# Weight combinations in small pieces, and eight units of the last product converted in the second layer

## The chip, the cores and the metric

One core of a Trainium2 chip runs the kernel. The metric is the device time of one execution in microseconds (us). Engines are called TensorE (PE in the profile; PEld is its weight load), VectorE (DVE), ScalarE (ACT), GpSimd (POOL) and SyncE (SP), whose queue issues the DMAs spoken of here.

## The reference

A retention layer feeds a two-layer network of 2304 tokens by 512 features:

```python
scores = scale * np.matmul(q, k.transpose(0, 1, 3, 2))     # 4 batches, 8 heads, 576 tokens, 64 features
x = np.matmul(scores * Dmat, v)                            # Dmat: gamma ** distance, causal
h = x @ w_in                                               # first layer, 512 -> 2048
x = (h * np.tanh(softplus(h))) @ w_out                     # mish, 2048 -> 512
g, val = x @ w_gate, x @ w_val                             # second layer, 512 -> 1536, twice
out = (g * (1 / (1 + np.exp(-g))) * val) @ w_out2          # 1536 -> 512, "the last product"
```

The inputs q, k and v are float32; the weights come as float64.

## The kernel before

**Numbers.** A float32 value is held as two parts, a rounded one and the rest, and a matrix product is three matmuls for each pair of tiles. The float64 weights are decoded on the chip. A raw tile (512 KB, 128 partitions of 512 doubles) is loaded, `rebias_raw` (L112) scales the high words on ScalarE (L114) and shifts the low ones on VectorE (L115), `sign` (L117, L119) and `join` (L121, L123) put them together on VectorE, and a cast on ScalarE and a subtraction on VectorE or GpSimd make the two parts (`part`, L125, for the first layer's units).

**Work of TensorE.** The tokens are six blocks of 384. After the retention (which already holds slots 0 to 3), the first layer runs blocks 0 to 3 in 64 *slots*, 16 to a block: a slot is 12 matmuls `g1` (L615) and, four slots later, 12 matmuls `g2` (L649) that add to four PSUM banks. At a block's end `g2_out` (L654, L659) copies the banks out, two on ScalarE and two on VectorE, before the next block may fill them. Blocks 4 and 5 go together through eight *pairs* (`pair1`, L888): two by two weight units are multiplied with seven block products instead of eight. A pair has seven *steps*; in a step one product (six matmuls, L813) is followed by some matmuls of waiting accumulations (L826, L855). The second layer runs all of its 18 *units* (three token pairs times six weight pairs) in this form, each with a gate half (z = 0) and a value half (z = 1) of seven steps (`strassen`, L1027), the accumulations of the last product (L989) in between. In a step the first product goes to a copy on ScalarE (L921 or L1061), and most of the others to an add on VectorE (L820) that reads the bank; two PSUM banks serve the three sums of a half in turn.

**Weights for it.** The seven products need combinations of weights: for a group of two weight units, four corner pieces a11 to a22 (128 x 256 x 2) and sums s1 to s4, of which seven are used. They are made while the first layer runs, and stored in device memory: `put` (L189) casts a piece on ScalarE (L191), subtracts on VectorE (L192) and stores (L193) from a pool "c" of four buffers. There are

- twelve groups of gate and value weights, `group(n)` (L203): load two raw tiles, decode, four sums (`combine`, L199, L201), seven stores into `comb`;
- eight groups of first-layer weights, `group1(i)` (L231): add the two parts of units that are there already (L246), four sums, four stores `e_s` and three straight from the units, into `ecomb`;
- twelve units of the last product, `last(i)` (L259): load, decode, two casts with subtractions on GpSimd, two stores into `find`, from which `fin_load` (L736) loads them in the second layer.

**Order.** The program is in the order in which it is written (no scheduler); each engine takes its instructions in turn. `pieces()` (L273) yields this work as 154 pieces, each made of whole stages (both rebiases of a group; three stores, then two, then two). `second` (L303) is called at the end of each slot from slot 20 on (L704) and of each step of the pairs (L942), and makes pieces until their number is 2.6 for each slot and 1.15 for each step. Raw tiles come from one ring of four buffers (`rp`). Functions in the list `ahead` split inputs of the next stage, one or two to a step; for the second layer from step 34 on. `stream1` and `stream` (L724, L734) load the combinations into a ring of weight tiles ahead of the products, six in the pairs and nine in the second layer.

Of the kernel before, what the change touches and what calls it, by code (L numbers as in the profile page):

```python
# [16 lines left out]
def retention_mish_swiglu(  # L17
# [34 lines left out]
    RATE, RATE1, AHEAD = 2.6, 1.15, 34  # L52
# [6 lines left out]
    rp = cr.enter_context(tc.tile_pool(name="rp", bufs=RAW, side="right"))  # L59
# [34 lines left out]
    def fetch(lim):  # L94
        j = stage[0]
        if j >= min(lim, len(todo)) or j - stage[3] >= RAW:
            return
        stage[0] += 1
        kind, i, src = todo[j]
        raw[j] = rp.tile([128, 2 * DM], U32, tag="raw", name=f"raw{j}")  # L100
        dst = raw[j] if kind in ("out", "fin") else raw[j].rearrange("p (k f) -> p k f", k=KT)
        nc.sync.dma_start(out=dst, in_=src)
# [81 lines left out]
    def raw_load(key, src, whole):  # L184
        raw[key] = rp.tile([128, 2 * DM], U32, tag="raw", name=f"raw{key}")
# [13 lines left out]
    def combine(v):  # L199
        for o, a, b, op in ADDS:  # L200
            nc.vector.tensor_tensor(out=v[o], in0=v[a], in1=v[b], op=op)  # L201

    def group(n):  # L203
# [4 lines left out]
        def load():  # L208
            for e in range(2):
                raw_load(keys[e], cols((w2_gate, w2_val)[z], 2 * i + e), False)  # L210

        def bias():
            for e in range(2):
                rebias_raw(keys[e])

        def whole(e):
            sign(keys[e])
            join(keys[e])
            lo, hi = words(keys[e])
            for h in range(2):  # L220
                v[f"a{e + 1}{h + 1}"] = lo[:, h * KH:(h + 1) * KH].bitcast(F32)
                v["s" + "1324"[2 * e + h]] = hi[:, h * KH:(h + 1) * KH].bitcast(F32)

        def puts(names):
# [4 lines left out]
        return load, bias, whole, lambda: combine(v), puts  # L229

    def group1(i):  # L231
        v = {}

        def whole():
            x = rp.tile([128, 2 * DM], U32, tag="raw", name=f"e{i}").bitcast(F32)
# [16 lines left out]
        def puts(names):  # L252
# [4 lines left out]
        return whole, lambda: combine(v), puts  # L257

    def last(i):  # L259
        key = f"f{i}"  # L260

        def whole():
            sign(key)
            join(key)
# [6 lines left out]
        return lambda: raw_load(key, rows(w2_out, i), True), lambda: rebias_raw(key), whole, puts  # L271

    def pieces():  # L273
        gr = [group(n) for n in range(2 * PAIRS)]
        yield gr[0][0]
        yield lambda: None
        for n in range(2 * PAIRS):
            load, bias, whole, sums, puts = gr[n]
            f_load, f_bias, f_whole, f_puts = last(n)
            g = group1(n) if n < F1 // 2 else None  # L280
            yield bias
            yield lambda: (whole(0), f_load())
            if g:
                yield g[0]
            yield lambda: whole(1)
            if g:
                yield g[1]
            yield sums
            yield lambda: puts(("a11", "a12", "a22"))
            if g:  # L290
                yield lambda: g[2](("s2", "s3"))
            yield lambda: puts(("s2", "s3"))
            yield lambda: (puts(("s1", "s4")), gr[n + 1][0]() if n + 1 < 2 * PAIRS else None)
            if g:
                yield lambda: g[2](("s1", "s4"))
            yield f_bias
            yield f_whole
            yield f_puts

    prep = pieces()  # L300
    made = [0]

    def second(lim):  # L303
        while made[0] < lim:
            made[0] += 1
            f = next(prep, None)
            if f is None:
                return
            f()
# [298 lines left out]
    with tc.manual_schedule():  # L608
# [70 lines left out]
        def slot(s):  # L679
# [23 lines left out]
            if s >= PREP:  # L703
                second(int((s + 1 - PREP) * RATE))  # L704
# [14 lines left out]
        ring2 = ring1[cut:] + ring1[:cut] + [("in", 9), None, None]  # L719
# [437 lines left out]
```

## Time and profile before

| | us |
|---|---|
| median of 3 runs (lowest to highest) | 936.55 (936.43 to 938.25) |
| the profiled execution | 935.03 |
| its span, first to last instruction | 933.2 |
| TensorE busy (share) | 910.6 (98%) |
| VectorE busy | 568.0 (61%) |
| ScalarE busy | 380.0 (41%) |
| GpSimd busy | 70.0 (8%) |
| granted clock, mean | 0.996 |

The profile is one execution, with every instruction's start and duration; a busy TensorE is not one at its peak, since matmuls overlap. "Idle before" an instruction is put down to the semaphore that came last. Stages by time from the span's start: retention to 105 us, slots to 361 us, pairs to 509 us, second layer to the end.

### The profile page before, as it was taken

To read this page: it belongs to the slowest core of one execution; us is meant where nothing else is said; L and a number is where in the kernel's file an instruction comes from. 1 tells how busy PE (TensorE), PEld (TensorE's weight loads), DVE (VectorE), ACT (ScalarE), POOL (GpSimd) and SP (SyncE) were. 2 spreads that over 40 slices of the span, in tenths; PEclk is the share of its full clock that TensorE was granted. 3 is DMA by queue.
4 is the path that set the end of the run, shared out by engine and by line. 5 is a ranking of instruction groups with operands and counts; after the bars stand their busy time and mean duration, and the time that the engine had idled before them with its cause. 6 is when DMAs were issued, how large, how long until landed. Compare 5 with 4: busy or idle time off the path is not lost.

```text
span 933.2 us, 15315 instructions
## 1 busy us (share of the span) xinstructions
PE 910.6 (98%) x5828; PEld 863.5 (93%) x5828; DVE 568.0 (61%) x1086; ACT 380.0 (41%) x798; POOL 70.0 (8%) x71
## 2 busy tenths in 40 slices
PE   9999999999999997999999999999999999999998
PEld 8888999999899997899999999999999999999997
DVE  3978599467767787777653544556544556544444
ACT  3877466355554555545443222223222223222222
POOL 3654100000000000000000000000000000000000
PEclk9999999999999999999999999999999999999999
DMA  9999265277776779989635666654644554644421
GB/s 219 258 251 219 74 199 176 62 237 230 254 255 213 240 251 303 317 300 321 216 125 216 242 203 204 203 168 154 227 163 159 157 164 156 228 158 158 159 68 67
DMA packets 130520, 185.97 MB, mean 199 GB/s; under 512 B 46736, under 2 KB 88464, under 8 KB 130448
## 3 DMA queue, kind: packets, MB, share of 16 engines
q1 hardware_dynamic: 129344, 184.58, 63.0%
q8 instruction: 46, 0.75, 0.3%
q10 hardware_dynamic: 1104, 0.42, 0.2%
q14 instruction: 26, 0.21, 0.1%
HBM read 137.26 MB, written 47.71 MB: 198 GB/s over the span
## 4 chain that ended last, share of the span: by engine, by line
PE 72%; DMA 10%; DVE 10%; ACT 4%; issue 2%; SPq 1%; POOL 0%; DVEq 0%; ACTq 0%; POOLq 0%
PE t L813 28%; PE fa L989 16%; PE h L615 7%; PE acc L649 6%; PE ea L855 5%; PE te L813 4%; DMA comb<-c 3%; DMA rawg<-in_moe_w_gate_dram 2%; DMA eu<-ecomb 2%; DMA rawv<-in_moe_w_val_dram 1%; PE o L518 1%; DMA raw<-in_moe_w_out_dram 1%; PE s L442 1%; DVE c L192 1%; DVE g L677 1%
## 5 line engine op out<-in xcount | busy, mean ns | idle before, releaser
L813 PE MATMUL t<-y,su 128*128 128x384 f32 x1512 | 306.3, 338 | 0.5 <-DVE cv L820 0.5
L813 PEld LDWEIGHTS t<-y,su 128*128 128x128 f32 x1512 | 270.6, 188 | 23.7 <-DVE cv L820 1.9
L989 PE MATMUL fa<-fu,g 128*128 128x512 f32 x648 | 190.3, 395 | 0.2 <-ACT g L1012 0.2
L615 PE MATMUL h<-xs,u 128*128 128x384 f32 x768 | 144.0, 337 | 0.7 <-DVE xs L325 0.7
L649 PE MATMUL acc<-g,u 128*128 128x384 f32 x720 | 135.0, 336 | 3.8 <-ACT y L659 3.5
L615 PEld LDWEIGHTS h<-xs,u 128*128 128x128 f32 x768 | 133.9, 188 | 1.5 <-DVE xs L325 1.0
L649 PEld LDWEIGHTS acc<-g,u 128*128 128x128 f32 x720 | 125.5, 188 | 5.2 <-ACT y L659 4.2
L989 PEld LDWEIGHTS fa<-fu,g 128*128 128x128 f32 x648 | 118.5, 188 | 7.8 <-ACT g L1012 0.5
L1012 ACT CAST g<-sg 128x384 fp32r<-128x384 f32 x72 | 36.9, 513 | 173.6 <-DVE sg L1048 120.3
L813 PE MATMUL te<-ye,eu 128*128 128x384 f32 x336 | 69.8, 343 | 9.3 <-ACT scratch L921 6.1
L855 PE MATMUL ea<-ge,u 128*128 128x256 f32 x576 | 78.1, 282 | 0.2 <-ACT y L659 0.2
L855 PEld LDWEIGHTS ea<-ge,u 128*128 128x128 f32 x576 | 75.6, 189 | 0.9 <-DVE y L659 0.4
L1037 ACT ACTIVATE sg<-sg 128x384 f32<-128x384 f32 x54 | 28.4, 525 | 100.1 <-DVE sg L820 100.1
L813 PEld LDWEIGHTS te<-ye,eu 128*128 128x128 f32 x336 | 57.5, 191 | 11.5 <-ACT scratch L921 6.4
L1017 DVE TENSOR_TENSOR g<-sg,g 128x384 fp32r<-128x384 f32 x72 | 40.2, 558 | 40.6 <-ACT g L1012 40.6
L677 DVE TENSOR_TENSOR g<-m,g 128x384 fp32r<-128x384 f32 x64 | 36.1, 565 | 36.7 <-ACT g L673 36.5
L820 DVE TENSOR_TENSOR u<-t,p 128x384 f32<-128x384 f32 x36 | 20.0, 556 | 48.0 <-PE t L813 43.6
L666 ACT ACTIVATE m<-h 128x384 f32<-128x384 f32 x64 | 31.0, 485 | 38.0 <-PE h L615 37.9
L820 DVE TENSOR_TENSOR v<-t,p 128x384 f32<-128x384 f32 x36 | 20.0, 556 | 41.9 <-PE t L813 41.2
L192 POOL TENSOR_TENSOR f<-rawf,f 128x256 fp32r<-128x256 f32 x24 | 18.9, 811 | 337.7 <-ACT f L191 267.2
L673 ACT CAST g<-m 128x384 fp32r<-128x384 f32 x64 | 32.9, 514 | 1.8
L1048 DVE TENSOR_TENSOR sg<-sg,cv 128x384 f32<-128x384 f32 x54 | 30.1, 558 | 1.9
(115 smaller groups left out, 991.7 us busy)
## 6 DMA issues: line engine op xcount, KB each, us to landing
su<-comb SPq DMA_DIRECT2D x126, 512.0 KB, 3.3
comb<-c SPq DMA_DIRECT2D x84, 256.0 KB, 2.4
eu<-ecomb SPq DMA_DIRECT2D x28, 512.0 KB, 5.4
raw<-in_moe_w_in_dram SPq DMA_DIRECT2D x16, 512.0 KB, 5.4
raw<-in_moe_w_out_dram SPq DMA_DIRECT2D x16, 512.0 KB, 3.9
ecomb<-e_s SPq DMA_DIRECT2D x32, 256.0 KB, 4.4
rawg<-in_moe_w_gate_dram SPq DMA_DIRECT2D x12, 512.0 KB, 6.2
rawf<-in_moe_w_out_dram SPq DMA_DIRECT2D x12, 512.0 KB, 6.0
```

The source lines that it names most:

```text
L615: nc.tensor.matmul(ps, lhsT=u[:, a, kk * 128:(kk + 1) * 128], rhs=s[:, e, :], start=(c == 0), stop=(c == n - 1),)
L649: nc.tensor.matmul(accs[b][d][:, :T], lhsT=u[:, a, d * 128:(d + 1) * 128], rhs=g[:, e, :], start=(i == 0 and c == 0), stop=(i == F1 - 1 an ...
L666: nc.scalar.activation(w, hs.pop(s), AF.Mish)
L673: nc.scalar.copy(out=gs[s][:, 0, :], in_=ws[s])
L677: nc.vector.tensor_tensor(out=g[:, 1, :], in0=ws.pop(s), in1=g[:, 0, :].bitcast(F32), op=ALU.subtract)
L813: nc.tensor.matmul(p, lhsT=w[:, a, kk * 128:(kk + 1) * 128], rhs=y[kk][:, x, :], start=begin and kk == 0 and (a, x) == (0, 0), stop=kk == ...
L820: nc.vector.tensor_tensor(out=out_, in0=a, in1=b_, op=ALU.add)
L855: nc.tensor.matmul(o, lhsT=u[:, a, d * 128:(d + 1) * 128], rhs=y, start=f == 0 and (a, x) == (0, 0) and (r == 0 or r == 2 and d % 2 == 0), ...
L989: nc.tensor.matmul(accs["f", b][m], lhsT=gs[u, e, h][:, x, m * 128:(m + 1) * 128], rhs=fu[2 * (u % PAIRS) + e][:, a, :], start=first, stop ...
L1012: nc.scalar.copy(out=gs[u, e, h][:, 0, :], in_=x)
L1017: nc.vector.tensor_tensor(out=g[:, 1, :], in0=x, in1=g[:, 0, :].bitcast(F32), op=ALU.subtract)
L1048: later.append(lambda: nc.vector.tensor_tensor(out=y, in0=y, in1=x, op=ALU.mult))
```

## The change

- The groups' work is dealt out by cost. Each piece has a cost (about its time on VectorE in us) and holds one conversion or at most two stores; `Pace` gives every slot or step a budget and makes pieces while the budget covers the next one's cost.
- Gate and value groups and `last` get 2.0 for each slot from 20, 1.2 from slot 51, and 1.2 for each step of pairs 1 to 7; none in pair 0. The groups of first-layer weights have a list of their own, 1.0 for each slot.
- The ring of raw tiles becomes four tiles with one buffer and one user each (two for a group, one for `last`, one for `group1`).
- Only units 0 to 3 of the last product are still made in the first layer (`FIRST = 4`). Units 4 to 11 are loaded raw in the second layer and converted by `fin_step` in the gate halves of units 1 to 4, one or two operations to a step, on VectorE and ScalarE, straight into their tiles. Behind groups 4 to 11 stand two empty pieces instead.
- The raw tiles of that take the place of a tile of the ring of weights (eight instead of nine). The split of inputs for the second layer starts at step 45 instead of 34, two to a step.

```diff
-    RATE, RATE1, AHEAD = 2.6, 1.15, 34
+    RATES, AHEAD = (2.0, 1.2, 1.2, 1.0), 45
...
-    def raw_load(key, src, whole):
-        raw[key] = rp.tile([128, 2 * DM], U32, tag="raw", name=f"raw{key}")
+    def raw_load(key, src, whole, n):
+        raw[key] = rp.tile([128, 2 * DM], U32, tag=f"raw{n}", name=f"raw{key}")
...
-        return load, bias, whole, lambda: combine(v), puts
+        return load, [
+            (0.55, lambda: rebias_raw(keys[0])), (0.55, lambda: rebias_raw(keys[1])),
+            (0.7, lambda: sign(keys[0])), (0.7, lambda: join(keys[0])),
+            (0.7, lambda: sign(keys[1])), (0.7, lambda: join(keys[1])),
+            (0.85, lambda: puts("a11", "a12")), (0.85, lambda: combine(v, ("s1", "s3"))),
+            (0.45, lambda: puts("a22")), (0.85, lambda: combine(v, ("s2", "s4"))),
+            (0.85, lambda: puts("s1", "s3")), (0.85, lambda: puts("s2", "s4")),
+        ]
...
-        return whole, lambda: combine(v), puts
+        return [
+            (1.4, whole), (0.85, lambda: combine(v, ("s1", "s3"))), (0.85, lambda: puts("s1", "s3")),
+            (0.85, lambda: combine(v, ("s2", "s4"))), (0.85, lambda: puts("s2", "s4")),
+        ]
+
+    FIRST = 4
...
+        gap = [(0.8, lambda: None)] * 2
+        for n, (load, steps_) in enumerate(gr):
+            f_load, behind = last(n) if n < FIRST else (None, gap)
+            if n == 0:
+                yield 0.0, load
+                yield from gap
+            yield from steps_[:2]
+            if f_load:
+                yield 0.0, f_load
+            yield from steps_[2:]
+            if n + 1 < len(gr):
+                yield 0.0, gr[n + 1][0]
+            yield from behind
+
+    class Pace:
+        def __init__(self, todo_):
+            self.todo, self.left, self.ahead = todo_, 0.0, next(todo_, None)
+
+        def __call__(self, more):
+            self.left += more
+            while self.ahead and self.left >= self.ahead[0]:
+                self.left -= self.ahead[0]
+                self.ahead[1]()
+                self.ahead = next(self.todo, None)
+
+    second = Pace(pieces())
+    third = Pace(x for i in range(F1 // 2) for x in group1(i))
...
-                second(int((s + 1 - PREP) * RATE))
+                third(RATES[3])
+                second(RATES[s >= NS - F1 + 3])
...
-        ring2 = ring1[cut:] + ring1[:cut] + [("in", 9), None, None]
+        ring2 = ring1[cut:] + ring1[:cut] + [None, None]
...
+        def fin_step(u, c):
+            n = FIRST + 2 * (u - 1)
+            i, k = divmod(c, 4) if c < 4 else (1, c - 3)
+            i += n
+            key = f"f{i}"
+            if k == 0:
+                rebias_raw(key)
+            elif k == 1:
+                sign(key)
+            elif k == 2:
+                join(key)
+                fin_load(i)
+                nc.scalar.copy(out=fu[i][:, 0, :], in_=words(key)[0].bitcast(F32))
+            else:
+                nc.vector.tensor_tensor(
+                    out=fu[i][:, 1, :], in0=words(key)[0].bitcast(F32), in1=fu[i][:, 0, :].bitcast(F32), op=ALU.subtract
+                )
+                fin_raw(i + 2)
+            if c == 3:
+                rebias_raw(f"f{n + 1}")
...
-                    pop(ahead, 1)
-                second(int((NS - PREP) * RATE + (step + 1) * RATE1))
+                    pop(ahead, 2)
+                if i:
+                    second(RATES[2])
...
-        fin_load(0)
-        fin_load(1)
+        for i in range(FIRST):
+            fin_load(i)
+        fin_raw(FIRST)
+        fin_raw(FIRST + 1)
...
+                if z == 0 and 0 < u <= (F2 - FIRST) // 2:
+                    fin_step(u, c)
```

ScalarE, slots 33 to 35, at the end of the second block of tokens, before. `m` and `g` are a slot's own mish and cast, `c` and `e_s` the casts of stores, `y` the block's copies out of PSUM:

```order
L666 ACTIVATE m_2888<-h_2863 128x384
L673 CAST g_2890<-m_2888 128x384
L191 CAST c_0_2893<-rawg_0_2691 128x256
L191 CAST c_2_2897<-rawg_0_2691 128x256
L191 CAST c_5_2901<-rawg_1_2693 128x256
L191 CAST e_s_2905<-e_2818 128x256
L191 CAST e_s_2909<-e_2818 128x256
L191 CAST c_1_2913<-rawg_1_2693 128x256
L191 CAST c_3_2917<-rawg_0_2691 128x256
L666 ACTIVATE m_2946<-h_2921 128x384
L673 CAST g_2890<-m_2946 128x384
L659 COPY y_2950<-acc_0_2251 128x384
```

The same place after:

```order
L661 ACTIVATE m_2900<-h_2875 128x384
L668 CAST g_2902<-m_2900 128x384
L191 CAST e_s_2905<-e_2713 128x256
L191 CAST e_s_2909<-e_2713 128x256
L191 CAST c_5_2915<-rawg_1_2737 128x256
L661 ACTIVATE m_2944<-h_2919 128x384
L668 CAST g_2902<-m_2944 128x384
L654 COPY y_2948<-acc_0_2251 128x384
L654 COPY y_2948<-acc_2_2253 128x384
L191 CAST c_4_2961<-rawg_0_2735 128x256
```

Seven casts for stores stood ahead of the block's copies, and three do now.

ScalarE at the entry into the pairs, before. `scratch` takes the first product of pair 0, `f` and `rawf` belong to a unit of the last product, `ye` to the pairs' inputs:

```order
L666 ACTIVATE m_4285<-h_4260 128x384
L673 CAST g_4235<-m_4285 128x384
L114 ACTIVATE rawf_4085<-rawf_4085 128x512
L191 CAST f_0_4293<-rawf_4085 128x256
L191 CAST f_1_4297<-rawf_4085 128x256
L921 COPY scratch<-te_1_4304 128x384
L766 CAST ye_0_4318<-x_1202 128x384
L766 CAST ye_1_4319<-x_1202 128x384
L114 ACTIVATE rawg_0_4246<-rawg_0_4246 128x512
```

And after:

```order
L661 ACTIVATE m_4199<-h_4174 128x384
L668 CAST g_4167<-m_4199 128x384
L114 ACTIVATE rawv_1_4099<-rawv_1_4099 128x512
L947 COPY scratch<-te_1_4209 128x384
L792 CAST ye_0_4223<-x_1202 128x384
L792 CAST ye_1_4224<-x_1202 128x384
L792 CAST ye_0_4245<-t_e 128x384
L792 CAST ye_1_4246<-t_e 128x384
L923 ACTIVATE we_4257<-te_1_4209 128x384
```

The unit of the last product is gone from ahead of the first product's copy, and the load's rebias from behind it.

VectorE in the gate half of unit 1 of the second layer, before (`u`, `v` and `sg` are the adds that read the banks):

```order
L820 TENSOR_TENSOR u_0_6053<-t_0_2_6044,p_0_6039 128x384
L820 TENSOR_TENSOR v_0_6076<-t_0_2_6044,p_0_6039 128x384
L820 TENSOR_TENSOR sg_11_6087<-t_0_3_6080,v_0_6076 128x384
L820 TENSOR_TENSOR sg_10_6101<-t_0_2_6044,p_0_6039 128x384
L820 TENSOR_TENSOR sg_01_6112<-t_0_3_6080,u_0_6053 128x384
```

And after:

```order
L846 TENSOR_TENSOR u_0_5944<-t_0_2_5935,p_0_5928 128x384
L119 SCALAR_TENSOR_TENSOR rawf_5657<-rawf_5657 128x512
L123 SCALAR_TENSOR_TENSOR rawf_5657<-rawf_5657 128x512
L846 TENSOR_TENSOR v_0_5971<-t_0_2_5935,p_0_5928 128x384
L760 TENSOR_TENSOR fu_5961<-rawf_5657,fu_5961 128x512
L115 TENSOR_SCALAR rawf_5659<-rawf_5659 128x512
L846 TENSOR_TENSOR sg_11_5987<-t_0_3_5980,v_0_5971 128x384
L119 SCALAR_TENSOR_TENSOR rawf_5659<-rawf_5659 128x512
L846 TENSOR_TENSOR sg_10_6002<-t_0_2_5935,p_0_5928 128x384
L123 SCALAR_TENSOR_TENSOR rawf_5659<-rawf_5659 128x512
L846 TENSOR_TENSOR sg_01_6016<-t_0_3_5980,u_0_5944 128x384
L760 TENSOR_TENSOR fu_6008<-rawf_5659,fu_6008 128x512
```

Conversions of two units (4 and 5) now stand between the adds.

## Rows read from the trace of the kernel before

**Rows 1.** The page, part 1: busy us (share of the span) and instructions.

```profile
PE 910.6 (98%) x5828; PEld 863.5 (93%) x5828; DVE 568.0 (61%) x1086; ACT 380.0 (41%) x798; POOL 70.0 (8%) x71
```

**Rows 2.** Windows by stage: us, busy us of engines (instructions), granted clock, DMA share, GB/s.

```profile
211.00:361.37 150.37, 146.12 (x837) 144.78 (x836) 115.82 (x251) 78.24 (x182) 9.33 (x12) 1.00 0.75 244
361.37:389.00 27.63, 19.83 (x98) 18.26 (x97) 20.12 (x44) 15.60 (x37) 1.44 (x2) 0.88 0.92 324
389.00:508.61 119.61, 117.95 (x834) 116.60 (x835) 73.73 (x153) 57.70 (x123) 6.54 (x8) 1.00 0.67 232
508.61:922.80 414.19, 413.45 (x2164) 383.77 (x2163) 201.71 (x377) 102.85 (x214) 0.00 (x0) 1.00 0.52 172
```

**Rows 3.** Waits of TensorE: us in total, times, longest us.

```profile
PE acc L649 <- ACT y L659: 3.5, 2, 2.1
```

**Rows 4.** Timeline, TensorE at the pairs' entry: start, us, what, count, [idle before].

```profile
361.37 1.21 PE L813 MATMUL te<-ye,eu 128*128 128x384 f32 x6
...
364.51 1.21 PE L826 MATMUL acc<-g,u 128*128 128x384 f32 x6
371.78 2.29 PE L813 MATMUL te<-ye,eu 128*128 128x384 f32 x6 [6.06 <-ACT scratch L921]
...
375.75 1.22 PE L813 MATMUL te<-ye,eu 128*128 128x384 f32 x6
...
388.91 1.32 PE L813 MATMUL te<-ye,eu 128*128 128x384 f32 x6 [0.31 <-DVE scratch L820]
```

**Rows 5.** Windows, the first 4 us after that wait (columns as in rows 2).

```profile
371.00:375.00 4.00, 3.22 (x10) 3.22 (x11) 2.56 (x6) 3.29 (x9) 1.44 (x2) 0.50 1.02 369
```

**Rows 6.** Timeline, ScalarE: fifth casts of two runs, and the pair's first copy.

```profile
240.60 0.41 ACT L191 CAST e_s<-e 128x256 fp32r<-128x256 f32 x1 [4.38 <-DMA comb<-c]
...
361.82 0.41 ACT L191 CAST e_s<-e 128x256 fp32r<-128x256 f32 x1 [4.91 <-DMA comb<-c]
...
371.26 0.47 ACT L921 COPY scratch<-te 128x384 f32<-128x384 f32 x1
```

**Rows 7.** The page, part 6, DMA issues: count, KB each, median us to landing.

```profile
su<-comb SPq DMA_DIRECT2D x126, 512.0 KB, 3.3
comb<-c SPq DMA_DIRECT2D x84, 256.0 KB, 2.4
...
rawg<-in_moe_w_gate_dram SPq DMA_DIRECT2D x12, 512.0 KB, 6.2
```

**Rows 8.** Timeline, SyncE, VectorE and TensorE in the pairs: loads and who waited.

```profile
395.21 0.43 DVE L115 TENSOR_SCALAR rawv<-rawv 128x512 uint32<-128x512 uint32 x1 [2.36 <-DMA rawv<-in_moe_w_val_dram]
...
410.41 1.48 SPq L186 DMA_DIRECT2D rawg<-in_moe_w_gate_dram  x2
...
416.82 0.43 DVE L115 TENSOR_SCALAR rawg<-rawg 128x512 uint32<-128x512 uint32 x1 [3.00 <-DMA rawg<-in_moe_w_gate_dram]
418.29 0.43 DVE L115 TENSOR_SCALAR rawg<-rawg 128x512 uint32<-128x512 uint32 x1 [1.04 <-DMA rawg<-in_moe_w_gate_dram]
...
419.24 1.32 PE L813 MATMUL te<-ye,eu 128*128 128x384 f32 x6 [1.16 <-DVE ve L820]
```

**Rows 9.** Groups by form: busy us, mean ns of one | idle before, releasers.

```profile
L123 DVE SCALAR_TENSOR_TENSOR rawf<-rawf 128x512 uint32<-128x512 uint32 x12 | 8.3, 693 | 0.4
...
L115 DVE TENSOR_SCALAR rawf<-rawf 128x512 uint32<-128x512 uint32 x12 | 5.0, 421 | 0.0
...
L134 DVE TENSOR_TENSOR u<-raw,u 128x512 fp32r<-128x512 f32 x19 | 13.0, 687 | 1.7 <-ACT u L133 0.9
...
L133 ACT CAST u<-raw 128x512 fp32r<-128x512 f32 x32 | 21.5, 672 | 14.1 <-DVE raw L123 13.9
...
L114 ACT ACTIVATE rawf<-rawf 128x512 f32<-128x512 f32 x12 | 8.1, 675 | 0.0
```

**Rows 10.** Windows, gate halves of units 3 and 4, and unit 4's value half.

```profile
575.00:586.60 11.60, 11.60 (x61) 10.76 (x61) 4.87 (x9) 2.63 (x6) 0.00 (x0) 1.00 0.78 247
...
598.20:609.80 11.60, 11.60 (x62) 10.77 (x61) 7.70 (x16) 3.38 (x8) 0.00 (x0) 1.00 0.80 251
609.80:621.40 11.60, 11.60 (x62) 10.79 (x61) 7.67 (x16) 2.74 (x6) 0.00 (x0) 1.00 0.48 156
```

More of the change, by code (lines that the diff above doesn't have):

```diff
@@ L99, in fetch @@
         kind, i, src = todo[j]
-        raw[j] = rp.tile([128, 2 * DM], U32, tag="raw", name=f"raw{j}")
+        raw[j] = rp.tile([128, 2 * DM], U32, tag=f"raw{j % RAW}", name=f"raw{j}")
         dst = raw[j] if kind in ("out", "fin") else raw[j].rearrange("p (k f) -> p k f", k=KT)
@@ L209, in load, with puts @@
             for e in range(2):
[L210 to L224, printed above, removed]
+                raw_load(keys[e], cols((w2_gate, w2_val)[z], 2 * i + e), False, e)
+                lo, hi = words(keys[e])
+                for h in range(2):
+                    v[f"a{e + 1}{h + 1}"] = lo[:, h * KH:(h + 1) * KH].bitcast(F32)
+                    v["s" + "1324"[2 * e + h]] = hi[:, h * KH:(h + 1) * KH].bitcast(F32)
+        def puts(*names):
             for nm in names:
@@ L234, in whole @@
         def whole():
-            x = rp.tile([128, 2 * DM], U32, tag="raw", name=f"e{i}").bitcast(F32)
+            x = rp.tile([128, 2 * DM], U32, tag="raw3", name=f"e{i}").bitcast(F32)
             for e in range(2):
@@ L277, in pieces @@
[L277 to L309, printed above, removed]
+        gap = [(0.8, lambda: None)] * 2
[11 more added lines that the diff above has]
+            yield from behind
@@ L738, in fin_load, with fin_raw @@
             fu[i] = place(*at_, [128, 2, DM], F32R, f"fu{i}")
-            nc.sync.dma_start(out=fu[i].bitcast(F32), in_=find[i])
+            if i < FIRST:
+                nc.sync.dma_start(out=fu[i].bitcast(F32), in_=find[i])
+        def fin_raw(i):
+            if i < F2:
+                key, shape = f"f{i}", [128, 2 * DM]
+                raw[key] = place("in", 9, shape, U32, f"raw{key}") if i % 2 else pools["rx"].tile(
+                    shape, U32, tag="rx", name=f"raw{key}"
+                )
+                nc.sync.dma_start(out=raw[key], in_=rows(w2_out, i))
+        def fin_step(u, c):
[14 more added lines that the diff above has]
+                    out=fu[i][:, 1, :], in0=words(key)[0].bitcast(F32), in1=fu[i][:, 0, :].bitcast(F32), op=ALU.subtract
+                )
+                fin_raw(i + 2)
+            if c == 3:
+                rebias_raw(f"f{n + 1}")
         def y_tile(n, c, k):
@@ L961, in retention_mish_swiglu @@
                 pop(ahead, len(ahead))
-            if i == 4:
+            if i == AHEAD // NG:
                 ya, yb = ysteps(0, x2t[0], x2t[1])
@@ L967, in retention_mish_swiglu @@
             ahead.pop(0)()
-        second(10 ** 6)
+        second(1000.0)
         cr.close()
         pools["sg"] = ctx.enter_context(tc.tile_pool(name="sg", bufs=5, side="right", reuse_waits="tile"))
+        pools["rx"] = ctx.enter_context(tc.tile_pool(name="rx", bufs=1, side="right", reuse_waits="tile"))
         pools["sx"] = ctx.enter_context(tc.tile_pool(name="sx", bufs=2, side="right", reuse_waits="tile"))
```

21 lines of the change are left out of this document (8 added, 13 removed).

## The prediction

> **What bounds the kernel now.** Read the page's first part first: TensorE is busy for 910.6 us of a span of 933.2 us [rows 1]. No other engine comes near, and the change alters neither number nor order of the 5828 matmuls. It can win only what TensorE idles or runs slowly, so the second view is the busy time by stage [rows 2]. The slots from 211.00 to 361.37 us lose 150.37 - 146.12 = 4.25 us. The entry into the pairs, 361.37 to 389.00, loses 7.80 us and has a granted clock of 0.88. The other seven pairs lose 1.66 us, and the second layer 0.74 us in 414. The other 8.2 us of idleness (22.6 less these) lie before 211 us and in the tail, where this change edits nothing.
>
> Third, who ends the idleness. In the slots the largest part is TensorE's wait for ScalarE's copies of a finished block out of PSUM, 3.5 us in two waits [rows 3]. Why ScalarE was late stands in its own timeline [rows 6]: at 240.60 a cast for a store had waited 4.38 us, and at 361.82 another 4.91 us, both for an earlier store to land. The pool "c" has four buffers, so the fifth cast of a run cannot start before the first of the run has been subtracted, issued and landed, and everything behind it in ScalarE's queue stands too. Behind the run of 361.82 stood the copy of the first pair product, done at 371.26 [rows 6]. TensorE waited for it.
>
> What that cost is counted from starts [rows 4]. Three groups of six matmuls take 364.51 - 361.37 = 3.14 us, 1.047 us each. From 361.37 to 388.91 there are 16 groups (eight products and the accumulations between them), which need 16.75 us and took 27.54 us: **10.8 us lost**. Of this 6.22 us are the wait itself (371.78 instead of 364.51 + 1.05), and about 1.9 us come after it, where the two groups from 371.78 to 375.75 took 3.97 us instead of 2.09 us: the granted clock there is 0.50, the 1.2 GHz level, after 6.06 us without a matmul [rows 4, 5]. The rest is a string of small waits for VectorE up to 388.91, while preparation work ran at full rate in the same steps.
>
> **The change part by part.**
>
> *Short runs.* Before, the seven casts of one slot (three, two and two stores from two kinds of group) stood in a row ahead of the block's copies; now there are three, and none in the last three slots ahead of the pairs' entry. Runs of four remain in eight slots and one of five in slot 23, but at the block ends, slots 35 and 51, they stand behind the copies; one, in slot 46, is ahead of an input's split. The 4.25 us go, and with each gap the refill that follows it: the wait of 6.06 us moved the starts by 6.22 us, so 0.16 us for each of three gaps, 0.5 us. Together 4.7 us. I leave 0.5 us as the price of the remaining runs of four (0, if the ring is clear by then, to 1.0 us, half of a block-end wait).
>
> *No preparation in pair 0.* The seven steps there now hold only their own work, and the last slots only one load and its first conversions. ScalarE's next job at the entry is then the copy itself. The 10.8 us go; what is next is the product's own chain (copy 0.47 us, an add of 0.55 us), which has a step of 2.09 us. Clock loss goes with the gap.
>
> *Preparation in pairs 1 to 7.* The 1.66 us there, with 0.16 us for each of some four gaps, are 2.3 us, made largely by loads: one issued at 410.41 was wanted by VectorE after 413.8, VectorE stood 3.00 and 1.04 us, and TensorE lost 1.16 us at 419.24; another hold of 2.36 us, at 395.21, cost TensorE nothing [rows 8]. The new plan has four gate or value loads left for this stretch (groups 8 to 11: the costs of all pieces add to 126.4, of which 31 x 2.0 + 13 x 1.2 = 77.6 are spent in the slots). Their lead is the two empty pieces, 1.6 at 1.2 a step, so 1.3 steps of 119.61 / 50 = 2.4 us: 3.2 us, against 6.2 us to landing [rows 7]. So VectorE will be held some 3 us at each, as before. Between 0 and 1.2 us each by those two rows; I take the middle, 0.6 us, so 2.4 us for four, with 0 and 4.8 us for the range. Queued behind the held conversion on VectorE is the next add that frees a PSUM bank. The preparation of the next layer's input now starts at step 45 with two pieces a step, and overlaps the last two steps of weight work; its ScalarE and VectorE pieces of 0.5 us are needed a pair later, so it is put at nothing, 0.5 us if that cover fails.
>
> *Eight units moved to the second layer.* Removed from the first layer: their loads, the 16 stores and part of the 14 us of VectorE work. Added in the second, for each unit on VectorE [rows 9]: shift 0.42, two joins 0.69 + 0.69 and the subtraction 0.69, 2.49 us; on ScalarE 0.68 + 0.67 = 1.35 us. Two units fall in one gate half: 4.98 us for VectorE, 2.7 us for ScalarE. A gate half lasts 11.60 us, with VectorE busy 4.87 us in it [rows 10], so it fills to 9.9 us and hides. Unit 4 also prepares the next block's inputs: 7.70 + 4.98 = 12.7 us in 11.60 us, which spills 1.1 us into the half behind it (7.67 us busy, 3.9 us free). An add has about one step, 11.60 / 7 = 1.66 us, until TensorE wants its bank, and lasts 0.56 us: 1.1 us of slack against 1.1 us of lateness. I take 0.5 us, 0 to 2. The raw loads are issued a whole unit (23 us) ahead, and the same bytes came in before as converted units; SyncE's queue waits once in a half for a subtraction, and the ring of weight tiles behind it, eight instead of nine, is 8 x 2 steps, 26 us, deep against 3.3 us for a load [rows 7]. Nothing for that.
>
> *Sum.* Recovered 4.7 + 10.8 + 2.3 = 17.8 us. Given back 0.5 + 2.4 + 0.5 = 3.4 us. Net **14.4 us**. The profiled execution took 935.03 us and would take 920.6 us; the median of the runs is 936.55 us, 1.5 us above it, and becomes **922.1 us**.
>
> **The rivals.**
>
> *A. The waits stay where groups are still made.* The load holds cost 1.2 us each (4.8 us), and a run of four stores ahead of one block end or input split still costs the 2.1 us that half of the 3.5 + refill was. For it: VectorE is 77% busy in the slots [rows 2], and one buffer for each load instead of a ring means that no load can start until the group before is stored. Against: three stores, not seven, ahead of the copies. Time: 936.55 - 17.8 + 4.8 + 2.1 + 0.5 + 0.5 = 926.7 us (925 to 930).
>
> *B. Nothing is given back.* The loads land sooner than 6.2 us, since 8 units of stores and loads have left the stretch, and a load of 512 KB in the second layer, with a DMA share of 0.52 instead of 0.67, lands in 3.3 us [rows 2, 7]. The lead of 3.2 us would then do: 936.55 - 17.8 = 918.8 us. The Trainium skill (DMA: Bandwidth & Descriptors, Latency and other measured facts) says that a lighter load on HBM makes the fixed part of a transfer smaller, which would make this case the likely one. The rows here compare reads of two different arrays, so they show a difference with the load but not its cause.
>
> *C. Slower.* VectorE in the second layer is the mechanism: conversions ahead of the adds delay every bank. If one piece of 0.69 us stood bare in each of the 28 steps, that were 19.3 us: 922.1 - 0.5 + 19.3 = 940.9 us. It decides from the point where VectorE comes to the adds over 1.1 us late in most steps, not in one half. Against: the order shows one piece between adds, rarely two, and three of the four halves fill to 85% only.
>
> *D. No gain.* Store waits do not come from the runs, but from the landing itself, and move into the pairs, so that ScalarE is as late as before: 936.6 us. Against: a store lands in 2.4 us [rows 7], and the waits of over 4 us begin only at the fifth cast.
>
> **How the numbers follow.** Forecast (920 to 925) 0.64, A 0.18, B 0.08, C 0.05, D 0.05. The time is the forecast's, 922.1 us. The range takes in A and B: 918 to 929 us, leaving out C, D and A's end. Differences of under 0.2% (1.9 us) cannot be told from none here. Faster: forecast, A and B, 0.90; same: D, 0.05; slower: C, 0.05.
>
> **What the profile will show.** Right, if TensorE's waits for ScalarE's block copies and for the first pair product are gone, the granted clock is 1.00 at the entry, the slots idle under 1 us, and the second layer's idle time stays under 2 us with VectorE some 20 us busier there. The step on the pairs is wrong if their idle time exceeds 5 us, and its row would name VectorE held by a load. The sum is wrong if the second layer loses more than 3 us to VectorE's adds, or if TensorE waits for a new thing at the entry into the second layer, where eight loads of 512 KB are now issued together.

## The result

The changed kernel takes **925.3 us** (median; 924.93 to 926.08), against 937.4 us for the kernel before, measured beside it: a ratio of 0.987 (95% interval 0.985 to 0.989). The forecast was 922.1 us with a range of 918 to 929: the sign and the range held. The gain, 11.3 us from the 936.55 us that the forecast started from (12.1 us from the 937.4 us beside it), was some 3 us smaller than the 14.4 us of the sum. The profiled execution took 924.93 us, with a span of 923.1 us.

First the page and TensorE's waits after the change (the page's first part: busy us, share of the span, instructions; the waits: us in total, times, longest us).

```profile
PE 906.4 (98%) x5828; PEld 862.3 (93%) x5828; DVE 564.0 (61%) x1094; ACT 379.5 (41%) x790; POOL 58.3 (6%) x55
```

```profile
PE te L839 <- DVE ve L846: 2.8, 2, 2.4
PE te L839 <- DVE scratch L846: 2.3, 2, 1.4
...
PE te L839 <- ACT we L923: 1.0, 1, 1.0
```

The wait for the block's copies [rows 3] and the wait for the first pair product [rows 4] are no longer among them. What stands there are waits for VectorE and ScalarE inside the pairs (`te`), 6.0 us in all (2.8 + 2.3 + 1.0 by these rounded rows, 6.01 by the third window of after below). Before, the pairs behind the entry held 1.66 us (the first window below).

Idle time alone hides slow starts, so the comparison goes by starts: the first matmul into `acc`, the first into `te`, the ninth group of `te` (16 groups later), the first into `t`, and the end of the last `t`. The stages of the two profiled executions, in us:

| stage | before | after | forecast | measured |
|---|---|---|---|---|
| up to the first `acc` | 107.52 | 108.56 | 0 | +1.04 |
| slots | 253.85 | 248.62 | -4.2 | -5.23 |
| entry into the pairs | 27.54 | 16.72 | -10.8 | -10.82 |
| pairs behind it | 112.63 | 116.44 | +0.1 | +3.81 |
| second layer | 421.26 | 422.30 | +0.5 | +1.04 |
| tail | 10.45 | 10.47 | 0 | +0.02 |
| span | 933.25 | 923.12 | -14.4 | -10.13 |

Windows by stage, before (the two stages that rows 2 doesn't show with these bounds) and after (us, then busy us and instructions of PE, PEld, DVE, ACT, POOL, then the granted clock, DMA share, GB/s):

```profile
388.91:501.53 112.62, 110.96 (x783) 109.61 (x784) 71.61 (x149) 54.50 (x118) 6.54 (x8) 1.00 0.67 229
501.53:922.80 421.27, 420.53 (x2215) 390.85 (x2214) 203.92 (x382) 106.15 (x219) 0.00 (x0) 1.00 0.53 174
```

```profile
211.00:357.18 146.18, 146.18 (x844) 146.18 (x842) 106.44 (x240) 77.10 (x179) 4.37 (x6) 1.00 0.71 240
357.18:373.93 16.75, 16.75 (x98) 16.75 (x98) 8.32 (x17) 7.96 (x18) 0.00 (x0) 1.00 0.35 115
373.93:490.34 116.41, 110.40 (x784) 109.39 (x783) 73.65 (x162) 51.80 (x116) 0.00 (x0) 1.00 0.68 224
490.34:912.65 422.31, 421.10 (x2215) 391.24 (x2214) 222.67 (x417) 117.33 (x239) 0.00 (x0) 1.00 0.52 173
```

In the slots PE is now busy for the whole window, as it is at the entry, at clock 1.00. The third row of after is where time went: 116.41 us with 110.40 us busy.

The entry after the change, in the timeline of ScalarE and TensorE (start, us, what, count, idle before in brackets):

```profile
357.18 1.21 PE L839 MATMUL te<-ye,eu 128*128 128x384 f32 x6
358.42 0.48 ACT L947 COPY scratch<-te 128x384 f32<-128x384 f32 x1 [1.51 <-PE te L839]
...
361.36 1.22 PE L839 MATMUL te<-ye,eu 128*128 128x384 f32 x6
```

The roles have changed: in rows 4 and 6 TensorE waited for ScalarE's copy, now ScalarE has waited 1.51 us for TensorE. The third `te` group starts 4.18 us after the first; before, it was 10.41 us (361.37 to 371.78, rows 4).

The loss in the pairs, in the timeline of SyncE's queue (SPq), VectorE, ScalarE and TensorE (other lines between these are left out):

```profile
385.07 3.48 SPq L193 DMA_DIRECT2D comb<-c  x4
387.31 0.76 DVE L192 TENSOR_TENSOR c<-rawv,c 128x256 fp32r<-128x256 f32 x2 [0.99 <-ACT c L191]
388.61 1.06 SPq L186 DMA_DIRECT2D rawg<-in_moe_w_gate_dram  x2
393.72 0.43 DVE L115 TENSOR_SCALAR rawg<-rawg 128x512 uint32<-128x512 uint32 x1 [3.49 <-DMA rawg<-in_moe_w_gate_dram]
395.31 0.43 DVE L115 TENSOR_SCALAR rawg<-rawg 128x512 uint32<-128x512 uint32 x1 [1.16 <-DMA rawg<-in_moe_w_gate_dram]
395.65 0.55 DVE L846 TENSOR_TENSOR scratch<-te,scratch 128x384 f32<-128x384 f32 x1
396.26 1.32 PE L839 MATMUL te<-ye,eu 128*128 128x384 f32 x6 [1.35 <-DVE scratch L846]
...
408.77 1.35 SPq L186 DMA_DIRECT2D rawv<-in_moe_w_val_dram  x2
414.65 0.43 DVE L115 TENSOR_SCALAR rawv<-rawv 128x512 uint32<-128x512 uint32 x1 [5.50 <-DMA rawv<-in_moe_w_val_dram]
414.70 0.67 ACT L114 ACTIVATE rawv<-rawv 128x512 f32<-128x512 f32 x1 [6.90 <-DMA rawv<-in_moe_w_val_dram]
415.81 1.33 PE L839 MATMUL te<-ye,eu 128*128 128x384 f32 x6 [0.96 <-ACT we L923]
...
430.04 1.68 SPq L186 DMA_DIRECT2D rawg<-in_moe_w_gate_dram  x2
436.12 0.43 DVE L115 TENSOR_SCALAR rawg<-rawg 128x512 uint32<-128x512 uint32 x1 [4.52 <-DMA rawg<-in_moe_w_gate_dram]
438.56 1.31 PE L839 MATMUL te<-ye,eu 128*128 128x384 f32 x6 [2.38 <-DVE ve L846]
...
452.86 1.04 SPq L186 DMA_DIRECT2D rawv<-in_moe_w_val_dram  x2
457.47 0.43 DVE L115 TENSOR_SCALAR rawv<-rawv 128x512 uint32<-128x512 uint32 x1 [3.61 <-DMA rawv<-in_moe_w_val_dram]
458.42 1.32 PE L839 MATMUL te<-ye,eu 128*128 128x384 f32 x6 [0.94 <-DVE scratch L846]
```

Four times the same chain: a raw load is issued, VectorE comes to its first conversion and stands, the add behind it in VectorE's queue stands too, and TensorE waits for the bank that this add frees. (At 415.81 it waits for ScalarE, which stood at the same load.) From the issue to the start of the conversion it is 5.11, 5.88, 6.08 and 4.61 us. VectorE wanted the tile at 393.72 - 3.49 = 390.23 us, 1.62 us after the issue; for the others the lead is 0.38, 1.56 and 1.00 us. The Trainium skill (Perfetto Trace Analysis, Tensor Engine Instruction (MATMUL, LD_WEIGHTS)) says that VectorE and ScalarE work strictly in turn; these rows agree: the add of 395.65 us comes only behind two conversions that waited 3.49 and 1.16 us.

The four waits of TensorE, 1.35 + 0.96 + 2.38 + 0.94 = 5.63 us, and one of 0.38 us at 452.98 us, behind a run of four casts of which the last had stood 2.95 us for a store, are the 6.0 us. The stage lost more than that: it takes 109.11 us when nothing waits, as the third experiment shows, so 116.44 - 109.11 = 7.33 us are lost, 1.3 us beyond the waits, or 0.26 us on the mean behind each of the five.

### The profile page after: what moved, and what is told of

Read it like the earlier page. It is cut to its first block, busy times and chain, and to the rows that moved or that the text cites. A ratio compares the mean times of both kernels' runs of the same rounds, so it can differ in the third digit from the quotient of the medians.

```text
span 923.1 us, 15226 instructions
## 1 busy us (share of the span) xinstructions
PE 906.4 (98%) x5828; PEld 862.3 (93%) x5828; DVE 564.0 (61%) x1094; ACT 379.5 (41%) x790; POOL 58.3 (6%) x55
## 4 chain that ended last, share of the span: by engine, by line
PE 82%; DMA 6%; DVE 6%; ACT 3%; issue 1%; SPq 1%; DVEq 0%; ACTq 0%
PE t L839 28%; PE fa L1019 16%; PE h L610 14%; PE acc L644 13%; PE te L839 3%; PE ea L881 3%; PE o L513 2%; DMA rawg<-in_moe_w_gate_dram 1%; DMA rawv<-in_moe_w_val_dram 1%; DMA q<-in_q_dram 1%; DMA raw<-in_moe_w_out_dram 1%; PE acc L852 1%; PE s L437 1%; DMA comb<-c 1%; PE o L504 1%
## 5 line engine op out<-in xcount | busy, mean ns | idle before, releaser
L123 DVE SCALAR_TENSOR_TENSOR raw<-raw 128x512 uint32<-128x512 uint32 x32 | 27.2, 851 | 0.0
```

## The experiments

Theory 1: casts in a row ahead of a copy made the waits at block ends and at the entry, and raw loads issued too late made those that are left; VectorE has room for the conversions in the second layer. The rivals are with each run. All kernels ran beside the kernel before, in two groups of runs (936 us for it in both); the 925.3 us of the changed kernel stand beside 937.4 us in a third. So differences of a few us are read from the stages and not from the medians alone.

**1. The pause alone**, in the kernel before: no preparation in pair 0, the combinations still in their long runs.

```diff
-                second(int((NS - PREP) * RATE + (step + 1) * RATE1))
+                if i:
+                    second(int((NS - PREP) * RATE + (step + 1 - NG) * RATE1))
```

> The kernel before with one edit: no weight work in the seven steps of pair 0, its count taken up again in pair 1 (the rest ends seven steps later, and overlaps the split of inputs that starts at step 34). Theory 1, runs of stores ahead in ScalarE's queue: the runs of seven and four in the last slots and the unit of the last product stay ahead of the first product's copy, so the wait of about 6 us at the pairs' entry stays; only the 2.4 us of small waits for VectorE inside pair 0 go: 934 to 936 us. Theory 2, the work inside pair 0 makes the loss: the whole 10.8 us go, 926 to 928 us.

Measured: 935.66 us, ratio 0.9996 (0.998 to 1.001): no change. TensorE and ScalarE at the entry, in the timeline, and the window behind the wait:

```profile
363.12 0.41 ACT L191 CAST e_s<-e 128x256 fp32r<-128x256 f32 x1 [4.90 <-DMA comb<-c]
...
371.91 0.74 ACT L191 CAST f<-rawf 128x256 fp32r<-128x256 f32 x2 [1.92 <-DVE rawf L123]
372.56 0.47 ACT L921 COPY scratch<-te 128x384 f32<-128x384 f32 x1
373.08 2.29 PE L813 MATMUL te<-ye,eu 128*128 128x384 f32 x6 [6.15 <-ACT scratch L921]
...
379.00 1.23 PE L826 MATMUL acc<-g,u 128*128 128x384 f32 x6
```

```profile
373.00:377.00 4.00, 3.92 (x12) 3.92 (x13) 2.84 (x6) 3.25 (x9) 0.90 (x2) 0.50 1.04 387
```

The fifth cast of a run waits 4.90 us for a store, the first copy comes late and TensorE waits 6.15 us, as in rows 4 and 6. The pause does shorten the entry, from 27.54 to 25.84 us, since the small waits in pair 0 are gone; but the pairs behind it grow from 112.63 to 114.83 us, where the same work now stands. So the pause moves waits of VectorE, and the long one belongs to what stands ahead of the copy. That is two things: the run, and behind it the unit of the last product, whose first operation starts at 369.33 us and whose casts end just before the copy at 372.56, 3.2 us later. This run does not tell them apart; run 4 shows the unit alone.

**2. Runs of seven put back** into the changed kernel: the costs of the pieces are kept, but a group's sums and its seven stores are each one piece.

```diff
-            (0.85, lambda: puts("a11", "a12")), (0.85, lambda: combine(v, ("s1", "s3"))),
-            (0.45, lambda: puts("a22")), (0.85, lambda: combine(v, ("s2", "s4"))),
-            (0.85, lambda: puts("s1", "s3")), (0.85, lambda: puts("s2", "s4")),
+            (1.7, lambda: combine(v, ("s1", "s3", "s2", "s4"))),
+            (0.45, lambda: puts("a11", "a12", "a22", "s1", "s3", "s2", "s4")), (2.55, lambda: None),
```

> The changed kernel with the four sums of a gate or value group in one piece and its seven stores in the next, at the cost of the piece they replace; so seven casts (nine with the two of a first-layer group) stand in slot 34 and seven in slot 50, right ahead of the slots in which a block's copies are made. Budgets, loads and everything else as in the change. Theory 1, runs of stores: TensorE waits again for the block's copies on ScalarE, 3.5 us in two waits, and more in the pairs: 928 to 931 us. Theory 2, it is the lower rate and not the short runs: slots without idle time, 925 to 926 us.

Measured: 939.55 us, ratio 1.004 (1.002 to 1.006): all of the gain is gone, far above the 928 to 931 us that theory 1 had said. The slots take 257.13 us instead of 248.62 and the pairs 121.36 instead of 116.44; the entry stays at 16.72 us. The end of the second block in the timeline of ScalarE and TensorE:

```profile
245.34 0.42 ACT L191 CAST c<-rawg 128x256 fp32r<-128x256 f32 x1 [1.02 <-DMA comb<-c]
...
248.02 0.85 ACT L653 COPY y<-acc 128x384 f32<-128x384 f32 x2
...
248.55 3.87 PE L643 MATMUL acc<-g,u 128*128 128x384 f32 x12 [4.21 <-ACT y L653]
```

Nine casts stand ahead of the block's copies here, and the wait for these is 4.21 us, twice the longest of rows 3. In the pairs there are five runs of seven, and behind each TensorE waits, 1.42 to 2.80 us; the casts wait there for stores, as at the block's end. So the short runs carry the gain in the slots. In the pairs the loss is 121.36 - 109.11 = 12.25 us (109.11 is the stage without a wait, run 3) against the changed kernel's 7.33, and its source is another: no wait of TensorE there stands behind a raw load. The entry stays whole: in this plan the run nearest to it ended at 353.5 us, 13 us ahead of the first `te`. So no run puts a long run right ahead of the entry into the changed kernel; that it made the long wait there rests on rows 6 and run 1, and on runs 4 and 5, which put back the other two suspects one by one.

**3. Two sets of raw tiles** in the changed kernel: groups 7, 9 and 11 have tiles of their own, and each load from group 8 on is issued as soon as the group ahead begins, not behind its stores.

```diff
-                raw_load(keys[e], cols((w2_gate, w2_val)[z], 2 * i + e), False, e)
+                raw_load(keys[e], cols((w2_gate, w2_val)[z], 2 * i + e), False, e + 2 * (n in (7, 9, 11)))
...
+            if 7 <= n < len(gr) - 1:
+                yield 0.0, gr[n + 1][0]
             yield from steps_[2:]
-            if n + 1 < len(gr):
+            if n < 7:
                 yield 0.0, gr[n + 1][0]
```

> The changed kernel with two sets of raw tiles for the groups that are made in the pairs: groups 7, 9 and 11 use the two tiles that the last product and the first-layer groups no longer need, and the load of each of groups 8 to 11 is issued at the start of the group before it, seven steps ahead instead of one. Theory 1, the pairs' idle time is VectorE and ScalarE held by loads that come too late: the waits of VectorE for gate and value loads vanish in the pairs, TensorE's idle time there falls from 6.0 us to under 1.5 us, and the time to 919.5 to 922 us. Theory 2, VectorE has too much to do in a step, whatever the loads: TensorE's idle time stays over 4 us and the time at 924 to 926 us.

Measured: **916.59 us**, ratio 0.980 (0.978 to 0.982), better than both kernels and below the 919.5 to 922 us expected. SyncE and VectorE in the timeline, and the window of the pairs behind the entry:

```profile
387.83 1.13 SPq L186 DMA_DIRECT2D rawv<-in_moe_w_val_dram  x2
...
406.18 0.76 DVE L115 TENSOR_SCALAR rawv<-rawv 128x512 uint32<-128x512 uint32 x2
```

```profile
372.66:481.75 109.09, 109.09 (x785) 109.09 (x784) 73.81 (x162) 51.16 (x116) 0.00 (x0) 1.00 0.70 230
```

The load has 18.35 us, the conversion has no idle time ahead of it, and the stage takes 109.11 us by starts, without a wait. VectorE is as busy as before the edit (73.81 against 73.65 us), and the runs of four are still there. So the 7.3 us that the changed kernel loses in the pairs come from the late loads (the 0.38 us behind a run of four went with them, and is not told apart). The slots (248.63), the entry (16.72) and the second layer (422.26) are as in the changed kernel; another 1.28 us between the two profiled executions lie ahead of the first `acc`, which the edit does not touch. The edit gives a load both an earlier place in SyncE's queue and, in part, tiles of its own; which of the two is needed is not told apart.

**4. All twelve units of the last product made in the first layer again**, in the changed kernel.

```diff
-    FIRST = 4
+    FIRST = 12
...
-        for i in range(FIRST):
-            fin_load(i)
-        fin_raw(FIRST)
-        fin_raw(FIRST + 1)
+        fin_load(0)
+        fin_load(1)
...
+            if u + 1 < PAIRS:
+                fin_load(2 * u + 2)
+                fin_load(2 * u + 3)
```

> The changed kernel with all twelve units of the last product made in the first layer as before (FIRST = 12; their loads in the second layer where they stood before): the second layer has no conversions, the pairs have four more units' conversions and stores, and the weight work ends some four steps later. Theory 1, the conversions in the second layer are hidden: its length stays within 0.6 us of the changed kernel's although VectorE is 20 us less busy there, and the pairs lose 1 to 4 us more: 926 to 929 us. Theory 2, the conversions cost the second layer 2 us or more: the second layer is that much shorter, and the time 922 to 925 us.

Measured: 925.9 us, ratio 0.990 (0.988 to 0.992), the same as the changed kernel with its 0.987 (0.985 to 0.989). Slots 248.67, entry 16.73, pairs 116.69 us: the 1 to 4 us more that were expected for the pairs did not come. That this stage comes out equal is in part chance, since its loss is made up otherwise: waits of 0.44, 0.75, 1.86 and 0.67 us, and a granted clock of 0.57 in the 4 us behind the third. ScalarE at the entry, in the timeline:

```profile
357.83 0.74 ACT L191 CAST f<-rawf 128x256 fp32r<-128x256 f32 x2 [1.23 <-DVE rawf L123]
358.70 0.48 ACT L947 COPY scratch<-te 128x384 f32<-128x384 f32 x1
```

A unit of the last product stands right ahead of the first copy again, and the copy still starts 1.25 us after the first `te` (357.45 us; 1.24 us in the changed kernel). So the unit alone, with no long run ahead of it, costs the entry nothing. The second layer takes 423.66 us, 1.36 more where up to 0.6 either way was expected, all of it at its entry (waits of 0.65 and 0.96 us, where the changed kernel has one of 0.57). Units 1 to 4, in whose gate halves the changed kernel makes its conversions, take 92.69 us by starts in both kernels: the conversions cost the second layer nothing.

**5. Without the pause**, in the changed kernel.

```diff
-                if i:
-                    second(RATES[2])
+                second(RATES[2])
```

> The changed kernel with the pace of the second raw weights left as it was before the change: their rate is constant through the pairs, with no pause after a group's stores. Theory 1 (the entry into the pairs waited because combinations ran in long rows ahead of the copy that TensorE wanted; the dealing out has removed the rows, so the pause is not needed for the entry): the wait for the first copies stays away, pair 0 may lose up to 2.4 us in small waits on VectorE, the four holds by a load keep their sum of about 5.6 us wherever they fall; 925 to 928 against 925.3 of the changed kernel. Theory 2 (the pause itself saved the entry): the entry loses about 10 us again, 934 to 936.

Measured: 928.44 us, ratio 0.991 (0.989 to 0.993), 3.1 us above the changed kernel. The first copies are not waited for, so theory 2 falls, and with it the pause as what saved the entry. But theory 1 had put the difference down to small waits, and it is a load again:

```profile
374.50 1.40 SPq L186 DMA_DIRECT2D rawg<-in_moe_w_gate_dram  x2
380.59 0.43 DVE L115 TENSOR_SCALAR rawg<-rawg 128x512 uint32<-128x512 uint32 x1 [4.31 <-DMA rawg<-in_moe_w_gate_dram]
383.01 1.32 PE L839 MATMUL te<-ye,eu 128*128 128x384 f32 x6 [2.85 <-DVE scratch L846]
...
426.31 2.29 PE L839 MATMUL te<-ye,eu 128*128 128x384 f32 x6 [2.68 <-DVE ve L846]
```

```profile
426.31:430.31 4.00, 4.00 (x17) 4.00 (x18) 3.93 (x8) 2.05 (x4) 0.00 (x0) 0.58 0.20 50
```

A hold costs more or less by the step into which it falls: the first one here 2.85 us, the four of the changed kernel 0.94 to 2.38. The hold at 426.31 us costs the clock too: the group behind it takes 2.29 us instead of 1.32, the granted clock of 4 us is 0.58 (a mean of its two levels), and the next `te` starts 3.70 us later (430.01 us), where after the changed kernel's wait of 2.38 us it was 2.21 us. That is 1.5 us more. The pairs behind the entry take 119.76 us instead of 116.44, the entry 17.25 instead of 16.72.

**6. More work for VectorE in the second layer**: the sign and the join of each unit converted there are made three times, the second and third time to no effect.

```diff
-                sign(key)
+                for _ in range(3):
+                    sign(key)
...
-                join(key)
+                for _ in range(3):
+                    join(key)
```

> The changed kernel with the sign and the join of each conversion in the second layer made three times instead of once (the extra ones write what stands there already): 8 more VectorE operations per unit, about 5.5 us. In a gate half of 11.6 us VectorE then has 4.87 + 4.98 + 5.5 = 15.4 us, in the half that was fuller 18.2 us. Theory 1 (the conversions cost nothing because VectorE has room left for them; a full engine is late at the adds that TensorE waits for): lateness of 3.8 us in a gate half against the 1.1 us of slack, so some 2.7 us lost in each of three such halves and 5.5 us in the fuller one: about 939. Theory 2 (the adds are never behind the conversions, or the emptier value halves take up the work): TensorE loses nothing there, 925 to 926.

Measured: 936.74 us, 11.4 us above the changed kernel (ratio 1.000 to the kernel before, 0.998 to 1.002). The windows of units 3 and 4, gate and value half each, by starts:

```profile
569.78:582.54 12.76, 12.25 (x62) 10.43 (x60) 11.49 (x21) 3.88 (x8) 0.00 (x0) 1.00 0.56 183
582.54:594.97 12.43, 11.93 (x60) 10.77 (x61) 8.02 (x14) 3.37 (x7) 0.00 (x0) 1.00 0.54 192
594.97:609.92 14.95, 12.29 (x62) 10.42 (x60) 13.73 (x26) 4.68 (x10) 0.00 (x0) 1.00 0.44 142
609.92:623.14 13.22, 12.22 (x60) 10.73 (x61) 11.04 (x21) 3.83 (x8) 0.00 (x0) 1.00 0.36 119
```

A half takes 11.59 us in the changed kernel. Here unit 3's take 12.76 and 12.43 us, a loss of 2.0 us, and unit 4's lose 5.0 us; the expectation had 2.7 and 5.5. So the account of VectorE's time holds: a full VectorE does delay the adds (TensorE waits 1.61 us for one at 605.06 us), and late work spills into the value half. What the change itself puts there stays under the point from which it costs, as the same two halves of unit 4 in the changed kernel show:

```profile
587.82:599.40 11.58, 11.58 (x61) 10.76 (x60) 10.57 (x22) 5.23 (x11) 0.00 (x0) 1.00 0.50 161
599.40:610.99 11.59, 11.59 (x61) 10.77 (x60) 8.68 (x18) 3.32 (x7) 0.00 (x0) 1.00 0.48 158
```

**7. Two sets, and the split for the second layer three steps earlier.** The changed kernel's entry into the second layer, in the timeline of ScalarE and TensorE:

```profile
492.90 0.92 ACT L792 CAST y<-y 128x384 fp32r<-128x384 f32 x2
...
493.84 1.28 ACT L1007 ACT_TABLE_LOAD   x1
495.14 0.48 ACT L1091 COPY p<-t 128x384 f32<-128x384 f32 x1
495.67 1.33 PE L839 MATMUL t<-y,su 128*128 128x384 f32 x6 [0.57 <-ACT p L1091]
```

TensorE waits 0.57 us for a copy that stands behind two casts of the split and a load of ScalarE's function table.

```diff
-    RATES, AHEAD = (2.0, 1.2, 1.2, 1.0), 45
+    RATES, AHEAD = (2.0, 1.2, 1.2, 1.0), 42
```

> The kernel with two sets of raw tiles, and the split of the second layer's input started three steps earlier. Theory 1 (the 0.57 us that TensorE waits at the entry into the second layer is ScalarE's chain of casts, a table load and a copy, which starts too late): the wait goes, 916.0 against 916.6. Theory 2 (the last product before it is what the chain waits for): 916.6 as without.

Measured: 916.3 us, ratio 0.979 (0.977 to 0.981); against 916.59 that is too little to tell from none. In the trace the wait is gone and the second layer takes 421.43 us instead of 422.26, 0.83 us less (the wait, and 0.26 us behind it); the stretch up to the first `acc`, which the edit does not touch, took 0.71 us more in this execution. The theory is borne out by the trace, not by the time.

**8. Two sets, without the pause** (the edit of 5 in the kernel of 3).

> The kernel with two sets of raw tiles, and the constant pace of the second raw weights through the pairs (no pause after a group's stores). Theory 1 (once a load is issued a whole group ahead, the pause only moves work of VectorE about): 916.6 within 0.5. Theory 2 (without the pause VectorE is late in the first pair): up to 2.4 us more, 919.

Measured: 918.25 us, ratio 0.981 (0.979 to 0.983), between the two theories: the entry takes 17.25 us instead of 16.72 and the pairs 109.67 instead of 109.11. So of the 3.85 us by which these two stages grow in run 5 (0.53 + 3.32) about 1.1 us belong to the work that the pause keeps out of pair 0 (one wait of 0.33 us at its end, and starts that run late around it). The rest hangs on the late loads, 1.5 us of it by way of the clock.

## Why the prediction was right in sign and range, and 3 us short

- **Block ends (4.7 us): right.** The slots lost 253.85 - 248.63 = 5.22 us before and lose none now; the 0.5 us kept for runs of four did not come up there. It came up in the pairs, as the one wait of 0.38 us. So the slots gave 1.0 us more than forecast (5.23 against 4.2), and by luck that hides a part of what the pairs lost.
- **Entry (10.8 us): right**, 10.82 us. Its division was nearly right: run 1 puts the small waits at 1.7 us; the wait and the clock after it are the other 9.1. The text named the run alone as what stood ahead of the copy; the unit of the last product added up to 3.2 us to a queue that was late already, and costs nothing where it is not (run 4).
- **Pairs 1 to 7: the failed step.** The forecast had 2.3 us recovered and 2.4 us given back, +0.1 in all; it was 3.52 (112.63 - 109.11) and 7.33, +3.81. The mechanism was named rightly, four holds with the next add queued behind each, and so was the sign of this step being wrong: over 5 us of idle time there, with VectorE held by a load. It is 6.01 us. Its size was wrong, and by the lead: I counted two empty pieces, 1.3 steps, 3.2 us between issue and use. The load stands in SyncE's queue behind the group's last stores, and these wait for VectorE's subtraction, which waits for its cast. (The second of the two raw tiles is itself read by these last subtractions, so its load could not have gone out before them on any queue.) In the first of the rows above the subtraction starts at 387.31 us and VectorE wants the tile at 390.23, 2.92 us later; but the load goes out at 388.61, and 1.62 us are left. That was the best of the four. With 4.6 to 6.1 us from issue to use, VectorE stood 3.5 to 5.5 us, not 3. The bound that I took from one row of before (1.16 us for 3.00 us of hold [rows 8]) was for a shorter hold; 4.52 us cost 2.38. The 2.3 us that I counted as recovered went by idle time, 1.66 us, which misses that matmuls also ran late.
- **Refill: mis-sized.** I took 0.16 us for each gap from one wait; here it is 0.26, which makes 0.5 us over five waits. That a wait of under 3 us can also cost the clock (run 5) was not in the sum; in the changed kernel it did not happen.
- **Second layer (0.5 us): right in sum, wrong in place.** The conversions that I charged 0.5 us cost nothing: units 1 to 4 take 92.69 us with and without them (run 4). The spill into unit 4's value half is there (VectorE 8.68 us busy in it, 7.67 before [rows 10]), and no add was late for it. The split, which I put at nothing with 0.5 us if its cover failed, lost its cover at the one point where ScalarE also loads a table: 0.57 and 0.26 us. That is the new wait at this entry which the prediction looked out for, and it is for ScalarE's copy, not for the loads.
- **Rival A** had nearly the right time (926.7 us) and half the right reason: the loads, not the runs. **B** is out: loads took 4.6 to 6.1 us, and the DMA share in the pairs is 0.68 against 0.67 [rows 2], so the rule of the Trainium skill named there (DMA: Bandwidth & Descriptors, Latency and other measured facts), on a lighter load, was not put to the test. **C** is out here, but run 6 shows that it is a real limit: 5.5 us more of VectorE's work in a unit cost it 2 to 5 us. **D** is out by the measured time, and by run 2, where the long runs alone bring the waits back.
- The median fell by 11.3 us (936.55 to 925.3), the profiled execution by 10.1. The difference lies in where the two profiled executions stand among the runs; 1.04 us of it shows up ahead of the first `acc`, which the change does not touch.

## What to carry to other kernels

Work that is dealt out beside a bound engine costs by its place in the queues: never put more of it in a row, ahead of what the bound engine wants, than the store buffers hold. A load's lead counts from where the issuing queue really gets to it, behind stores that wait for other engines, and not from its line in the program; a second set of tiles with loads a whole group ahead was worth 7.3 us here. To compare two traces, cut them at the starts of the same matmuls: idle time alone showed 1.66 us of the 3.52 us that the pairs lost before.

## What the runs showed of the hardware

- After 6.15 us without a matmul the clock was at its 1.2 GHz level: three groups took 5.92 us (373.08 to 379.00), and the granted clock of the first 4 us is 0.50 (run 1). After shorter waits both came up: after 2.38 us (438.56 us, changed kernel) and 2.85 us (383.01 us, run 5) the next group took 1.31 and 1.32 us, and the granted clock of the 4 us behind was 1.00; after 1.86 us (465.45 us, run 4), 2.68 us (426.31 us, run 5) and 2.80 us (460.79 us, run 2) it was 0.57, 0.58 and 0.59, with groups of 1.97, 2.29 and 2.29 us. So the length of one wait does not settle it in these runs.
- The table load of ScalarE lasted 1.28 us, and the copy behind it started 0.02 us after its end. The Trainium skill (ScalarE: Activation LUTs, What ACT_TABLE_LOAD costs) gives about 1.28 us for the load, as here, and another 1.38 us for a drain; the rows have no room for that, 0.02 us ahead of it and 0.02 behind it, so 1.3 us is its price here.
- What a hold of VectorE costs TensorE does not follow its length: 0.94 us for 3.61 us of hold and 2.85 us for 4.31 us (run 5), but 0.96 us for 5.50 us, where the wait that ended last was for ScalarE.
